# Copying accumulators out of PSUM in their own column order, and undoing the order in the addresses of the stores

## The chip, the cores and the metric

The kernel runs on one core of one Trainium2 chip. The metric is the device time of one launch in microseconds (us). Before the change it is 2262.58 us, the median of three runs (2262.18 to 2262.81).

## The reference, cut to what matters

A light convolution (each of 8 heads has 7 softmaxed taps, applied backwards in time to its 24 channels) is followed by a feed-forward layer with a piecewise quadratic activation:

```python
# x: (8, 4096, 192), weight: (8, 7), w_in: (192, 2048), w_out: (2048, 192), float32
w = softmax(weight, axis=-1)
x_unf = x_pad[:, idx, :].reshape(B, S, K, H, group)          # 7 taps per token
x = einsum('hk,bskhg->bshg', w, x_unf).reshape(B * S, 192)   # 32768 tokens
h = x @ w_in
g = where(h >= 1, h, where(h <= -1, 0, (h + 1) ** 2 / 4))
out = g @ w_out                                              # (32768, 192)
```

## The kernel before, in words

**Tiling.** The 32768 tokens are cut into 64 strips of 512 (TB). The 2048 hidden channels are cut into 8 pairs of 128-channel blocks (NPAIR). A step q is one pair in one strip, so a strip has 8 steps and there are 512 of them. Two strips share one round of the convolution, so the work repeats every 16 steps.

**A step.** The loop over q writes the order of each engine by hand (manual schedule). TensorE (PE) does `mm1(q)`, 18 matmuls on half the rows each, into a double-buffered PSUM tile h; then `mm2(q-2)`, 20 matmuls into the accumulators of its strip. Operands are split into a high and a low part, so mm2 reads two tiles, gh and gl. Between them VectorE (DVE) does `act_clip(q)` (L473), `act_lo(q-1)` (L497, makes gl) and `act_max(q)` (L484); ScalarE (ACT) does `act_hi(q-1)` (L491, makes gh) and `act_square(q)` (L479). The convolution of the strips to come is laid between these: products on ACT (L219), sums on GpSimd (POOL, L230), transpositions on DVE (L147).

**Four accumulators, one set.** A strip sums into four PSUM tiles: accm0 and accm1 for output channels 0 to 127, accr0 and accr1 for channels 128 to 191; the index is the half of the rows that was summed. There is one set, since the pool has one buffer of each. When the last step of a strip has been through mm2, `evac` copies the four tiles to SBUF tiles t on ACT (L513), in the order accm0, accm1, accr0, accr1, and POOL adds each pair (L515). The first mm2 of the next strip writes the same tiles, first accm (8 matmuls from gh, then 4 from gl), then accr. In ACT's own queue the four copies stand behind `act_square` of their step and ahead of `act_hi` of the next.

**Token order.** mm1 and mm2 each read their moving operand by turns from the first and second half of a strip, so the columns of an accumulator are permuted. Column 4a + 2b + o holds token 256b + 128o + a. From strip 2 on (`in_turns`) the copy on ACT undoes this: it reads a PSUM tile in order and writes t with steps of 128 and 256 elements.

**Storing.** Two and three steps into the next strip, `store` transposes the summed tile by blocks of 32 x 32 on DVE into osb (L538) and issues 4 stores for "m" and 2 for "r" from the sync engine's queue (SP, L542), 64 KB each in runs of 32 floats. SP also issues, in the same queue, the loads of x (L95) and the copies that swap partition halves of the convolution's result (L235, L236). Strips 0 and 1 are computed and stored in another way, and strip 63 is emptied by `evac_last`; neither is touched.

Of the kernel before, what the change touches and what calls it, by code (L numbers as in the profile page):

```python
# [20 lines left out]
SQ = 32  # L21
# [9 lines left out]
def lightconv_then_ffn(ctx: ExitStack, tc: tile.TileContext, x, weight, w_in, w_out, out):  # L31
# [24 lines left out]
    nc = tc.nc  # L56
# [343 lines left out]
    def in_turns(s):  # L400
        return s * NPAIR >= NF32
# [99 lines left out]
    def evac(s):  # L501

        acc = accs.pop(s)
        n = slice(0, 2 * D if s * NPAIR < NF32 else TB)
        for a in "mr":
            t = [ob.tile([P, TB], F32, name="t", bufs=4) for _ in range(2)]
            y = ob.tile([P, TB], F32, name="sum")
            for i in range(2):
                to, of = t[i][:, n], acc[a, i][:, n]
                if in_turns(s):  # L510
                    to = to.rearrange("p (b o a) -> p a b o", b=2, o=2)
                    of = of.rearrange("p (a b o) -> p a b o", b=2, o=2)
                nc.scalar.copy(to, of)  # L513
            if s > 0:
                nc.gpsimd.tensor_add(y[:, n], t[0][:, n], t[1][:, n])  # L515
            else:
                late.append((y[:, n], t[0][:, n], t[1][:, n]))
            sums[s, a] = y
# [9 lines left out]
    def store(s, a, *engs):  # L528
        engs = engs or (nc.sync,)
        y = sums.pop((s, a))  # L530
        if s * NPAIR < NF32:
            t0 = s * TB + (0 if a == "m" else 2 * P)
            engs[0].dma_start(out=out[t0:t0 + 2 * P].rearrange("(b p) d -> p b d", p=P),
                              in_=y[:, 0:2 * D].rearrange("p (b d) -> p b d", b=2))
            return
        n = P if a == "m" else DR
        osb = ob.tile([P, TB // SQ, SQ], F32, name="osb")
        nc.vector.transpose(out=osb[0:n].rearrange("p j b -> p (j b)"), in_=y[0:n])  # L538
        for i in range(n // SQ):
            c0 = i * SQ + (0 if a == "m" else P)  # L540
            dst = out[s * TB:(s + 1) * TB, c0:c0 + SQ]
            engs[i % len(engs)].dma_start(out=dst.rearrange("(j a) b -> a j b", a=SQ),  # L542
                                          in_=osb[i * SQ:(i + 1) * SQ])

    def diagonal(t, *bases):
        nc.gpsimd.memset(t, 0.0)
# [293 lines left out]
    for q in range(NQ + DELAY):  # L840
        s, j = divmod(q, NPAIR)
        c, i = divmod(q, 2 * NPAIR)
# [20 lines left out]
        else:  # L863
            if q - 1 in gs:
                act_hi(q - 1)
            if q == NPAIR + 1:
                evac(0)
# [19 lines left out]
            if q < NQ and j == m:  # L887
                evac_rest(s - 1)
                store(s - 1, "m")
            elif q < NQ and j == r:  # L890
                store(s - 1, "r")
# [31 lines left out]
```

## Time and profile before

| what | value |
|---|---|
| median of 3 runs | 2262.58 us |
| the profiled execution | 2263.56 us |
| its span, first to last instruction | 2261.8 us |
| granted TensorE clock | 1.000 |
| busy DVE, ACT, POOL | 92%, 79%, 51% of the span |
| DMA | 110.84 MB, mean 49 GB/s |

The span is what the traces cover; 1.76 us of the profiled execution lie around it. Times in the timelines are us from the start of the span. "PEld" is the loading of TensorE's weights, which runs ahead of the matmuls; a wait of PEld is the matmul's wait seen at its weights. Matmul ends are modelled, so the starts are the figures to use.

### The profile page before, as it was taken

The page shows a single profiled execution, that of the slowest core. Times are in us where ns is not written, and L with a number is a line of the kernel's source. Part 1 is how long each engine was busy: PE and PEld are TensorE (multiplying, and loading weights), DVE is VectorE, ACT ScalarE, POOL GpSimd, SP SyncE. Part 2 cuts the span into 40 slices and gives each one's busy share as a digit, 9 for nine tenths or more (in the row PEclk, how much of TensorE's full clock was granted, in tenths as well). Part 3 has the DMA queues.
Part 4 walks back from the last instruction along what each step waited for, and adds up shares of the span by engine and source line. Part 5 has one row for each costly group of instructions (what it writes and reads, how often), then busy time and mean ns, then how long its engine had stood idle before and what let it go on. Part 6 is the DMA issues. An engine that isn't in the chain of part 4 may idle for free.

```text
span 2261.8 us, 48144 instructions
## 1 busy us (share of the span) xinstructions
PE 2189.4 (97%) x19646; PEld 1862.2 (82%) x19646; DVE 2077.1 (92%) x1883; ACT 1785.3 (79%) x2153; POOL 1148.6 (51%) x868
## 2 busy tenths in 40 slices
PE   9999999999999999999999999999999999999999
PEld 6988888888888888888888888888888888888887
DVE  8899999999999999999999999999999999999998
ACT  7787877778877788777887787877878778788775
POOL 1455644556545565444654455644556445565451
PEclk9999999999999999999999999999999999999999
DMA  6222122221222212222122222222221222212211
GB/s 158 49 51 51 38 53 44 47 53 38 51 48 46 53 34 51 49 49 51 41 44 48 49 50 48 42 48 44 51 53 39 51 49 45 54 34 51 49 32 27
DMA packets 442125, 110.84 MB, mean 49 GB/s; under 512 B 410288, under 2 KB 417840, under 8 KB 441904
## 3 DMA queue, kind: packets, MB, share of 16 engines
q1 hardware_dynamic: 441744, 107.66, 24.2%
q8 instruction: 155, 2.54, 0.5%
q14 instruction: 66, 0.54, 0.1%
q10 hardware_dynamic: 160, 0.10, 0.0%
HBM read 32.84 MB, written 25.17 MB: 26 GB/s over the span
## 4 chain that ended last, share of the span: by engine, by line
DVE 26%; ACT 23%; PE 20%; issue 14%; POOL 12%; SPq 3%; DMA 1%; POOLq 0%; DVEq 0%; ACTq 0%
POOL y L230 11%; PE h L422 9%; DVE g L484 8%; ACT t L513 8%; DVE g L473 8%; DVE gl L497 7%; ACT g L479 6%; ACT gh L491 5%; PE accm L462 5%; PE accr L462 4%; DVE osb L538 2%; SPq L95 2%; ACT p L219 2%; POOL lo L252 2%; DMA raw<-in_x_dram 1%
## 5 line engine op out<-in xcount | busy, mean ns | idle before, releaser
L230 POOL TENSOR_TENSOR y<-y,p 128x512 f32<-128x512 f32 x546 | 799.8, 1465 | 757.9 <-DVE g L484 539.8
L497 DVE TENSOR_TENSOR gl<-g,gh 128x1024 fp32r<-128x1024 f32 (+1 forms) x497 | 727.5, 1464 | 151.4 <-ACT gh L491 140.4
L491 ACT CAST gh<-g 128x1024 fp32r<-128x1024 f32 (+1 forms) x497 | 519.2, 1045 | 253.9 <-DVE g L484 248.7
L422 PE MATMUL h<-hi,w 64*128 64x512 f32 x4032 | 701.6, 377 | 0.0
L479 ACT ACTIVATE g<-g 128x1024 f32<-128x1024 f32 (+1 forms) x505 | 533.6, 1057 | 161.3 <-DVE g L473 151.0
L462 PE MATMUL accm<-gh,w 64*128 64x512 f32 x3968 | 614.0, 381 | 48.0 <-ACT t L513 48.0
L484 DVE TENSOR_TENSOR g<-h,g 128x1024 f32<-128x1024 f32 (+1 forms) x505 | 613.4, 1215 | 8.2 <-ACT g L479 4.4
L473 DVE TENSOR_SCALAR g<-h 128x1024 f32<-128x1024 f32 (+1 forms) x505 | 604.8, 1198 | 11.6 <-PE h L422 10.8
L422 PEld LDWEIGHTS h<-hi,w 64*128 64x128 f32 x4032 | 522.7, 186 | 50.5
L462 PEld LDWEIGHTS accm<-gh,w 64*128 64x128 f32 x3968 | 439.1, 186 | 128.4 <-ACT t L513 78.3
L422 PE MATMUL h<-lo,w 64*128 64x512 f32 x2016 | 541.7, 376 | 0.0
L462 PE MATMUL accr<-gh,wr 64*128 64x512 f32 x1984 | 390.4, 382 | 15.7 <-ACT t L513 15.7
L462 PE MATMUL accm<-gl,w 64*128 64x512 f32 x1984 | 380.0, 382 | 3.2
L219 ACT ACTIVATE p<-xT,wk 128x512 f32<-128x512 f32 x562 | 375.1, 710 | 0.0
L462 PE MATMUL accr<-gl,wr 64*128 64x512 f32 x1984 | 374.1, 376 | 0.0
L422 PEld LDWEIGHTS h<-lo,w 64*128 64x128 f32 x2016 | 330.4, 186 | 25.8
L462 PEld LDWEIGHTS accr<-gh,wr 64*128 64x128 f32 x1984 | 251.9, 186 | 63.0 <-ACT t L513 40.2
L422 PE MATMUL h<-rhi,w 64*128 64x512 f32 x992 | 293.6, 376 | 0.0
L422 PE MATMUL h<-rh,w 64*128 64x512 f32 x992 | 293.5, 376 | 0.0
L462 PEld LDWEIGHTS accm<-gl,w 64*128 64x128 f32 x1984 | 248.6, 186 | 44.3 <-DVE gl L497 23.1
L462 PEld LDWEIGHTS accr<-gl,wr 64*128 64x128 f32 x1984 | 256.8, 186 | 26.1 <-DVE gl L497 0.2
L515 POOL TENSOR_TENSOR sum<-t 128x512 f32<-128x512 f32 (+1 forms) x124 | 158.5, 1279 | 153.3 <-ACT t L513 153.3
(141 smaller groups left out, 2008.6 us busy)
## 6 DMA issues: line engine op xcount, KB each, us to landing
out_dram<-osb SPq DMA_DIRECT2D x366, 64.0 KB, 1.9
raw<-in_x_dram SPq DMA_DIRECT2D x334, 68.0 KB, 2.4
hi<-hi SPq DMA_DIRECT2D x126, 128.0 KB, 2.3
lo<-lo SPq DMA_DIRECT2D x126, 128.0 KB, 2.3
rhi<-rh SPq DMA_DIRECT2D x62, 128.0 KB, 2.2
rlo<-rl SPq DMA_DIRECT2D x62, 128.0 KB, 2.3
words<-in_moe_w_in_dram SPq DMA_DIRECT2D x16, 192.0 KB, 4.0
words<-in_moe_w_out_dram SPq DMA_DIRECT2D x8, 384.0 KB, 4.0
```

Of the source, the lines that this page charges most:

```text
L95: (engs[i] if engs else nc.sync).dma_start(out=raw[i * SQ:(i + 1) * SQ, lo:n // SQ + 1, :], in_=src.rearrange("(j a) b -> a j b", a=SQ),)
L219: nc.scalar.mul(p, self.xT[:, SH + k:SH + k + TB], wk[:, self.wsel, k:k + 1])
L230: nc.gpsimd.tensor_add(y, y, self.product(k))
L422: nc.tensor.matmul(to, w[HALVES[e], c0:c0 + P], of, start=(n == 0), stop=(n == len(mms) - 1))
L462: nc.tensor.matmul(both(accs[s][a, i]), st, turns(g[HALVES[i], e, :]), start=(j == 0 and n == first[a]), stop=(j == NPAIR - 1 and n == las ...
L473: nc.vector.tensor_scalar(out=g[:, e, :], in0=hs[q][:, e, :], scalar1=-1.0, scalar2=1.0, op0=ALU.max, op1=ALU.min)
L479: nc.scalar.activation(g[:, e, :], g[:, e, :], AF.Square, bias=0.5, scale=0.5)
L484: nc.vector.tensor_tensor(out=g[:, e, :], in0=h[:, e, :], in1=g[:, e, :], op=ALU.max)
L491: nc.scalar.copy(gh[:, e, :], gs[q][:, e, :])
L497: eng.tensor_sub(gl[:, e, :], g[:, e, :], gh[:, e, :])
L513: nc.scalar.copy(to, of)
L515: nc.gpsimd.tensor_add(y[:, n], t[0][:, n], t[1][:, n])
```

## The change

The copies out of PSUM no longer rearrange: they read 512 columns and write 512 columns, both in order. The sum, the small add in `evac_rest` and the 32 x 32 transposition therefore work on permuted tokens. With a = 8j + k (k from 0 to 7, j from 0 to 15) and e = 2b + o, column 4a + e is column 4k + e of transposition block j, so partition 4k + e of osb holds, in block j, token 128e + 8j + k. The address of the store is written in those terms.

```diff
             for i in range(2):
-                to, of = t[i][:, n], acc[a, i][:, n]
-                if in_turns(s):
-                    to = to.rearrange("p (b o a) -> p a b o", b=2, o=2)
-                    of = of.rearrange("p (a b o) -> p a b o", b=2, o=2)
-                nc.scalar.copy(to, of)
+                nc.scalar.copy(t[i][:, n], acc[a, i][:, n])
...
             dst = out[s * TB:(s + 1) * TB, c0:c0 + SQ]
-            engs[i % len(engs)].dma_start(out=dst.rearrange("(j a) b -> a j b", a=SQ),
-                                          in_=osb[i * SQ:(i + 1) * SQ])
+            engs[i % len(engs)].dma_start(
+                out=dst.rearrange("(e j k) b -> k e j b", e=4, k=SQ // 4),
+                in_=osb[i * SQ:(i + 1) * SQ])
```

No instruction is added, removed or moved on any engine. What differs is the shape of 244 copies on ACT (128x128x4 before, 128x512 now) and of 366 stores on SP. The rows below are SP's queue in the middle of a round of two strips, before: two swaps of the low part (lo), the stores of a strip, then the swaps of the remaining channels (rh, rl).

```order
L235 DMA lo_2523<-lo_2517 64x512
L236 DMA lo_2523<-lo_2517 64x512
L542 DMA out_dram<-osb 32x16x32 x6
L235 DMA rhi<-rh 64x512
L236 DMA rhi<-rh 64x512
L235 DMA rlo<-rl 64x512
```

The same place with the change:

```order
L235 DMA lo_2523<-lo_2517 64x512
L236 DMA lo_2523<-lo_2517 64x512
L538 DMA out_dram<-osb 8x64x32 x6
L235 DMA rhi<-rh 64x512
L236 DMA rhi<-rh 64x512
L235 DMA rlo<-rl 64x512
```

The order is the same. The address side of a store was 32 rows of 16 runs, and is now 8 rows (k) of 64 runs, since e and j together form one even step of 8 tokens; each run is 32 floats in both. The osb side stays 32 partitions of 512 floats.

## The prediction

> **What bounds the kernel now.** I read the busy row first, then the table of waits, then the timeline of one round of two strips.
>
> ```profile
> PE 2189.4 (97%) x19646; PEld 1862.2 (82%) x19646; DVE 2077.1 (92%) x1883; ACT 1785.3 (79%) x2153; POOL 1148.6 (51%) x868
> ```
>
> PE is the bound by this row, and DVE is close behind. ACT, on which the copies run, has room on average. What matters is where PE stops:
>
> ```profile
> DVE gl L497 <- ACT gh L491: 140.4, 106, 2.2
> ...
> PEld accm L462 <- ACT t L513: 78.3, 91, 1.2
> ...
> PEld accr L462 <- ACT t L513: 40.2, 61, 0.7
> PEld accm L462 <- DVE gl L497: 23.1, 58, 0.5
> ```
>
> The copies (L513) hold up the weight loads of mm2 for 78.3 + 40.2 = 118.5 us: the next strip cannot start before the four accumulators are copied. The 61 waits for accr are one per strip change that the change touches (strips 2 to 62). The copies also stand ahead of gh in ACT's queue, and most of DVE's idle time, 140.4 us, is waiting for gh.
>
> One round, PE. The first row opens the step in which a new strip begins (I call this strip change A); then the two restarts, and the openings of the next two steps.
>
> ```profile
> 1001.83 0.81 PE L422 MATMUL h<-hi,w 64*128 64x512 f32 x4
> 1004.66 1.13 PE L462 MATMUL accm<-gh,w 64*128 64x512 f32 x7 [0.41 <-ACT t L513]
> 1006.48 0.70 PE L462 MATMUL accr<-gh,wr 64*128 64x512 f32 x3 [0.26 <-ACT t L513]
> 1007.23 0.80 PE L422 MATMUL h<-hi,w 64*128 64x512 f32 x4
> 1011.33 0.80 PE L422 MATMUL h<-hi,w 64*128 64x512 f32 x4
> ```
>
> An undisturbed step takes 1011.33 - 1007.23 = 4.10 us. Step A takes 5.40: 1.30 are lost. The other strip change of the round (B), eight steps on:
>
> ```profile
> 1036.70 0.59 PE L422 MATMUL h<-hi,w 64*128 64x512 f32 x4
> 1039.60 0.48 PE L462 MATMUL accm<-gh,w 64*128 64x512 f32 x1 [0.80 <-ACT t L513]
> 1040.51 1.13 PE L462 MATMUL accm<-gh,w 64*128 64x512 f32 x7 [0.42 <-ACT t L513]
> 1042.32 0.70 PE L462 MATMUL accr<-gh,wr 64*128 64x512 f32 x3 [0.25 <-ACT t L513]
> 1043.07 0.80 PE L422 MATMUL h<-hi,w 64*128 64x512 f32 x4
> 1071.78 0.81 PE L422 MATMUL h<-hi,w 64*128 64x512 f32 x4
> ```
>
> Step B takes 6.37, so 2.27 are lost. From A to the next A are 1071.78 - 1001.83 = 69.95 us, where 16 undisturbed steps would take 65.6. Of the 4.35 us lost, 3.57 are at A and B; the rest, about 0.8, lies in the heavy half between them, where DVE is late with gl:
>
> ```profile
> 1022.85 0.30 PEld L462 LDWEIGHTS accm<-gl,w 64*128 64x128 f32 x4 [0.53 <-DVE gl L497]
> ```
>
> **The copies.** Groups of copies on ACT, by shape: count, busy us and mean ns.
>
> ```profile
> L513 ACT COPY t<-accr 128x512 f32<-128x512 f32 x122 | 123.0, 1113 | 0.0
> L513 ACT COPY t<-accm 128x512 f32<-128x512 f32 x122 | 118.9, 1079 | 0.0
> ...
> L202 ACT COPY hi<-accm 128x512 f32<-128x512 f32 x1 | 0.6, 586 | 1.4 <-PE accm L181 1.4
> ...
> L198 ACT COPY rh<-accr 128x512 f32<-128x512 f32 x1 | 0.6, 572 | 0.0
> ```
>
> L202 and L198 are the operation that the change makes of L513: a copy of 512 floats from PSUM to SBUF, both sides in order. They take 0.58 us against 1.10. Only two samples, but strip 0 copies its accumulators in order too, 384 columns wide, at a time when PE runs:
>
> ```profile
> 58.51 0.83 ACT L513 COPY t<-accm 128x384 f32<-128x384 f32 x2
> 59.24 0.86 ACT L513 COPY t<-accr 128x384 f32<-128x384 f32 x2
> 60.02 1.06 ACT L479 ACTIVATE g<-g 128x1024 f32<-128x1024 f32 x1
> ```
>
> Four take 1.51 us from start to start, 0.38 each for some 0.47 of duration: neighbours overlap by about 0.1. So four of 0.58 should take 4 x 0.485 = 1.94 us. At A and B the rows now are:
>
> ```profile
> 1002.66 1.95 ACT L513 COPY t<-accm 128x512 f32<-128x512 f32 x2
> 1004.42 2.01 ACT L513 COPY t<-accr 128x512 f32<-128x512 f32 x2
> 1006.23 1.05 ACT L491 CAST gh<-g 128x1024 fp32r<-128x1024 f32 x1
> ...
> 1038.51 1.95 ACT L513 COPY t<-accm 128x512 f32<-128x512 f32 x2
> ```
>
> Today four take 1006.23 - 1002.66 = 3.57 us, so each strip change gives ACT 1.63 us back. Bounds for a copy: 0.57 (L198) and 1.11 (no change); I take 0.58.
>
> **What PE gets at A.** A step is 38 matmuls in 4.10 us, 0.108 each, so mm1 (18) is over, and accm wanted, 1.94 us after the step opens: 1003.77. The second copy will end at 1002.66 + 0.49 + 0.58 = 1003.73, so accm is free just in time. accr is wanted 12 matmuls (1.29 us) later, at 1005.06; the fourth copy ends at 1002.66 + 3 x 0.485 + 0.58 = 1004.70. All 1.30 us go. This is tight for accm: 0.1 us more per copy would bring 0.15 us of the wait back at each A.
>
> **What PE gets at B.** The copies start late here, at 1038.51, as ACT is kept by convolution work. accm is wanted at 1036.70 + 1.94 = 1038.64; the second copy ends at 1038.51 + 0.49 + 0.58 = 1039.58, with some 0.06 until PE moves. About 1.0 us stays, and 1.27 go. Everything ahead of B will have moved up together by then, so the lateness of ACT at B stays as it is. accr is then no longer late.
>
> **What DVE gets.** Its rows behind A and B, and POOL's sums at A:
>
> ```profile
> 1007.31 1.55 DVE L497 TENSOR_TENSOR gl<-g,gh 128x1024 fp32r<-128x1024 f32 x1 [1.91 <-ACT gh L491]
> ...
> 1011.66 2.31 DVE L497 TENSOR_TENSOR gl<-g,gh 128x1024 fp32r<-128x1024 f32 x1
> ...
> 1043.15 1.56 DVE L497 TENSOR_TENSOR gl<-g,gh 128x1024 fp32r<-128x1024 f32 x1 [2.01 <-ACT gh L491]
> ...
> 1004.68 1.28 POOL L515 TENSOR_TENSOR sum<-t 128x512 f32<-128x512 f32 x1 [2.89 <-ACT t L513]
> 1006.50 1.28 POOL L515 TENSOR_TENSOR sum<-t 128x512 f32<-128x512 f32 x1 [0.54 <-ACT t L513]
> ```
>
> gh comes 1.63 us sooner, inside both waits (1.91, 2.01), so DVE moves forward too. Not by all of it: gl takes 2.31 where POOL works beside it and 1.55 where the second sum covers its first 0.47 us. The sums also move up, to about 1003.8 and 1005.1, and the second will cover some 0.7 us of gl: I charge 0.15, and leave DVE 1.5. That is 0.2 more than PE's 1.30, and takes 0.2 from the wait for gl in the heavy half. The sums themselves, the transposition and the small add keep their sizes; nobody waits for them sooner.
>
> **The stores.** Six per strip, still 64 KB in 512 runs of 32 floats; only the addresses' steps differ. I cost them at nothing. Their landing is covered by the time until the same osb buffer is written again, one strip (35 us); their issue by the gaps in SP's queue. Bounds: unchanged, or, if 8 rows were worse than 32, a few times the landing and the issue of now; the price without cover is the last rival below.
>
> **Sum.** Per round 1.30 + 1.27 + 0.2 = 2.77 us; 61 strip changes are 30.5 rounds, 84.5 us. 2263.56 - 84.5 = 2179.1 for the profiled execution; the median shown is 0.98 below it, so **2178 us**.
>
> **Rivals.** *The sums cost DVE more.* If gl is slowed at each strip change to the longest row, 2.31 instead of 1.55, DVE keeps only 1.63 - 0.76 = 0.87 and PE must follow: 61 x 0.87 = 53, 2210 us. For it: DVE is 92% busy. Against: the overlap worked out is short. Chance 0.15.
>
> *All of the loss goes.* DVE's lead grows until ACT is on time at B and gl on time in the heavy half. PE would run 16 undisturbed steps: 4.35 x 30.5 = 133, 2130 us at best. The round's busy row speaks against the full sum:
>
> ```profile
> 1002.66:1072.66 70.00, 67.74 (x612) 57.46 (x611) 64.72 (x57) 55.82 (x68) 37.03 (x29) 1.00 0.24 47
> ```
>
> DVE (third figure behind the length) needs 64.72 of the 65.6, and still waits a little for gh. I put this case at 2130 to 2160. Chance 0.15.
>
> *The copies stay slow.* The price may be in the reading while PE writes other banks, not in the scattered writing. Then nothing moves: 2262. Strip 0's copies speak against it. [...] Chance 0.05.
>
> *Slower: stores that hold the transfer engines.* The swaps of rh and rl are issued behind the stores in the same queue and must land before mm1 of the next round:
>
> ```profile
> 1046.49 5.94 SPq L542 DMA_DIRECT2D out_dram<-osb  x6
> ...
> 1059.72 0.59 SPq L236 DMA_DIRECT2D rlo<-rl  x1
> ...
> 1065.30 0.38 PE L422 MATMUL h<-rl,w 64*128 64x512 f32 x1
> ...
> out_dram<-osb SPq DMA_DIRECT2D x366, 64.0 KB, 1.9
> ...
> rlo<-rl SPq DMA_DIRECT2D x62, 128.0 KB, 2.3
> ```
>
> The last swap lands at 1060.31 + 2.3 = 1062.6, 2.7 us before its matmul. The last store is issued by 1052.43; were it to hold the engines beyond 1065.30 - 2.3 = 1063.0, that is 10.6 us after its issue instead of 1.9, the swap behind it would be late for PE. Each us beyond costs 31 us, once a round, and from 2178 + 31 x 2.7 on, at 13.3 us, the kernel is slower than before (2283 at 14 us). Issue is no danger by itself: at twice the 5.94 us SP would be done at 1058.4, still some 2 us inside the swaps' margin. What the new shape could do to the landing: if the 512 runs went over half of the 16 engines, each would carry 64 and not 32, and twice 1.9 is 3.8 us, far from 10.6. The page "DMA: Bandwidth & Descriptors" (section Why a DMA increments its semaphore by 16 and not by 1) says that a copy uses the largest number of engines up to 16 that divides the slowest dimension of both sides: 16 for 32 rows, 8 for 8 rows; no row of before shows a store of 8 rows. Chance 0.03.
>
> **How the numbers follow.** The forecast has 0.62, within 2165 to 2195. With the cases of more (2130 to 2160) and of less (2195 to 2225), a range of 2143 to 2215 leaves out some 0.2. A difference of 0.2%, some 4.5 us, is about what a measurement of this kernel can tell from none. Faster 0.92, same 0.05, slower 0.03.
>
> **What would show it.** The copies at 0.58 us, and ACT's busy time down by 244 x 0.52 = 127 us; accr no longer waiting for t, accm still for about 1.0 us at every B (some 30 us); the wait of gl for gh down from 140 by up to 1.63 x 61 = 99; a round of 67.2 us; the stores' landing under 4 us. It would be wrong if the copies stayed above 0.8 us, if gl behind the strip changes took over 2 us, or if B kept or lost its whole wait.

## The result, and the profile after

The changed kernel takes **2169.9 us** (median of four runs, 2169.37 to 2170.33), against 2262.69 for the kernel before on the same chip: a ratio of 0.959 with a 95% interval of 0.9573 to 0.9606. It is 92.8 us faster, of which the prediction had 84.5. The profiled execution took 2170.33 us and has a span of 2168.6.

First the busy row of the profile after. The row has the same columns as the one of before:

```profile
PE 2153.0 (99%) x19646; PEld 1875.8 (86%) x19646; DVE 2084.0 (96%) x1883; ACT 1684.8 (78%) x2153; POOL 1139.4 (53%) x868
```

PE now stops for 1% of the span instead of 3%, with as many instructions as before. DVE has come up to 96%. ACT lost 100.5 us of work. The table of waits, after (engine, tile and line, whom it waited for: us in total, times, longest):

```profile
DVE gl L497 <- ACT gh L491: 41.3, 110, 0.6
...
PEld accm L462 <- ACT t L509: 29.4, 58, 0.7
...
PEld accm L462 <- DVE gl L497: 12.3, 54, 0.3
```

The 40.2 us of accr waiting for a copy have no row any more. accm's wait fell from 78.3 to 29.4, DVE's for gh from 140.4 to 41.3. The groups of copies by shape, after:

```profile
L509 ACT COPY t<-accr 128x512 f32<-128x512 f32 x122 | 66.4, 606 | 0.0
L509 ACT COPY t<-accm 128x512 f32<-128x512 f32 x122 | 64.5, 580 | 0.0
```

So 580 and 606 ns stand where 1079 and 1113 stood. PE's timeline at the strip change A, at B, and the step behind each, after:

```profile
962.73 0.81 PE L422 MATMUL h<-hi,w 64*128 64x512 f32 x4
...
964.67 1.24 PE L462 MATMUL accm<-gh,w 64*128 64x512 f32 x8
...
966.83 0.80 PE L422 MATMUL h<-hi,w 64*128 64x512 f32 x4
...
995.94 0.59 PE L422 MATMUL h<-hi,w 64*128 64x512 f32 x4
...
998.37 1.61 PE L462 MATMUL accm<-gh,w 64*128 64x512 f32 x8 [0.32 <-ACT t L509]
...
1000.90 0.80 PE L422 MATMUL h<-hi,w 64*128 64x512 f32 x4
```

Step A takes 966.83 - 962.73 = 4.10 us: nothing is lost there now. Step B takes 1000.90 - 995.94 = 4.96: 0.86 of its 2.27 remain. ACT's timeline at the two places:

```profile
963.55 1.06 ACT L509 COPY t<-accm 128x512 f32<-128x512 f32 x2
964.49 1.10 ACT L509 COPY t<-accr 128x512 f32<-128x512 f32 x2
965.45 1.08 ACT L491 CAST gh<-g 128x1024 fp32r<-128x1024 f32 x1
...
995.80 1.03 ACT L491 CAST gh<-g 128x1024 fp32r<-128x1024 f32 x1
996.78 1.06 ACT L479 ACTIVATE g<-g 128x1024 f32<-128x1024 f32 x1
997.75 1.05 ACT L509 COPY t<-accm 128x512 f32<-128x512 f32 x2
```

Four copies take 965.45 - 963.55 = 1.90 us from start to start. At B they start 997.75 - 995.94 = 1.81 us after the step opens, exactly as late as before (1038.51 - 1036.70). DVE's timeline, first behind A, then in the heavy half, then around B:

```profile
966.56 1.75 DVE L497 TENSOR_TENSOR gl<-g,gh 128x1024 fp32r<-128x1024 f32 x1 [0.26 <-ACT gh L491]
...
971.10 2.12 DVE L497 TENSOR_TENSOR gl<-g,gh 128x1024 fp32r<-128x1024 f32 x1
...
995.54 1.21 DVE L473 TENSOR_SCALAR g<-h 128x1024 f32<-128x1024 f32 x1
...
1000.75 2.04 DVE L497 TENSOR_TENSOR gl<-g,gh 128x1024 fp32r<-128x1024 f32 x1 [0.39 <-ACT gh L491]
```

gl waits 0.26 and 0.39 us for gh where it waited 1.91 and 2.01, but it takes longer itself: 1.75 instead of 1.55 behind A, 2.04 instead of 1.56 behind B. One round, by engine, after (the columns are those of the prediction's row: the stretch and its length, then the busy us of PE, PEld, DVE, ACT and POOL with their instructions, the clock, the DMA share and GB/s):

```profile
962.73:1029.61 66.88, 66.55 (x611) 57.55 (x609) 64.88 (x57) 52.45 (x67) 36.59 (x29) 1.00 0.26 49
```

A round is 66.9 us instead of 69.95, with DVE busy for 64.88 of them: its idle time per round has gone from 70.00 - 64.72 = 5.28 to 66.88 - 64.88 = 2.00 us.

### The profile page after: what moved, and what is told of

Its sections match the earlier page's. It is cut to its first block, busy times and chain, and to the rows that moved or that the text cites. A ratio compares the mean times of both kernels' runs of the same rounds, so it can differ in the third digit from the quotient of the medians.

```text
span 2168.6 us, 48144 instructions
## 1 busy us (share of the span) xinstructions
PE 2153.0 (99%) x19646; PEld 1875.8 (86%) x19646; DVE 2084.0 (96%) x1883; ACT 1684.8 (78%) x2153; POOL 1139.4 (53%) x868
## 3 DMA queue, kind: packets, MB, share of 16 engines
q1 hardware_dynamic: 438816, 107.65, 25.9%
## 4 chain that ended last, share of the span: by engine, by line
DVE 27%; PE 24%; ACT 19%; POOL 13%; issue 13%; SPq 3%; DMA 1%; POOLq 0%; DVEq 0%; ACTq 0%
POOL y L230 11%; PE h L422 10%; DVE g L484 9%; DVE g L473 8%; PE accm L462 7%; DVE gl L497 7%; ACT g L479 6%; ACT gh L491 5%; PE accr L462 4%; ACT t L509 4%; DVE osb L534 2%; SPq L95 2%; ACT p L219 2%; POOL lo L252 2%; DMA raw<-in_x_dram 1%
## 5 line engine op out<-in xcount | busy, mean ns | idle before, releaser
L497 DVE TENSOR_TENSOR gl<-g,gh 128x1024 fp32r<-128x1024 f32 (+1 forms) x497 | 734.4, 1478 | 51.6 <-ACT gh L491 41.3
L479 ACT ACTIVATE g<-g 128x1024 f32<-128x1024 f32 (+1 forms) x505 | 535.1, 1060 | 167.3 <-DVE g L473 157.0
L473 DVE TENSOR_SCALAR g<-h 128x1024 f32<-128x1024 f32 (+1 forms) x505 | 604.7, 1198 | 11.6 <-PE h L422 10.6
L462 PE MATMUL accm<-gh,w 64*128 64x512 f32 x3968 | 604.2, 378 | 9.3 <-ACT t L509 9.1
L422 PEld LDWEIGHTS h<-hi,w 64*128 64x128 f32 x4032 | 523.7, 186 | 47.9
L462 PEld LDWEIGHTS accm<-gh,w 64*128 64x128 f32 x3968 | 449.4, 186 | 77.0 <-ACT t L509 29.4
L462 PE MATMUL accr<-gh,wr 64*128 64x512 f32 x1984 | 373.4, 376 | 0.0
L462 PEld LDWEIGHTS accm<-gl,w 64*128 64x128 f32 x1984 | 250.9, 186 | 33.4 <-DVE gl L497 12.3
L462 PEld LDWEIGHTS accr<-gh,wr 64*128 64x128 f32 x1984 | 257.3, 186 | 24.7 <-ACT gh L491 0.2
L422 PEld LDWEIGHTS h<-rhi,w 64*128 64x128 f32 x992 | 184.5, 186 | 14.9
```

What stands on the lines that cost most here:

```text
L422: nc.tensor.matmul(to, w[HALVES[e], c0:c0 + P], of, start=(n == 0), stop=(n == len(mms) - 1))
L462: nc.tensor.matmul(both(accs[s][a, i]), st, turns(g[HALVES[i], e, :]), start=(j == 0 and n == first[a]), stop=(j == NPAIR - 1 and n == las ...
L473: nc.vector.tensor_scalar(out=g[:, e, :], in0=hs[q][:, e, :], scalar1=-1.0, scalar2=1.0, op0=ALU.max, op1=ALU.min)
L479: nc.scalar.activation(g[:, e, :], g[:, e, :], AF.Square, bias=0.5, scale=0.5)
L497: eng.tensor_sub(gl[:, e, :], g[:, e, :], gh[:, e, :])
```

## The experiments

Three questions were put: whether the gain is all of the copies and nothing of the stores; what it is in a copy that costs; and why B still loses 0.86 us, since the prediction had given a reason for that ("ACT is kept by convolution work") that no row had proved.

The table gives, for every version, the median, the ratio to the kernel before on the same chip with its interval, and where a round stands: the lengths of step A, of the two late steps of the heavy half, of step B, and of the round. The steps are read from the starts of mm1 in PE's weight queue, in one round between 960 and 1100 us, so they may differ by 0.02 from the matmul rows above. Rounds differ little, but for B in e6, where both of its lengths are given.

| kernel | median us | ratio | A | heavy | heavy, 2nd | B | round |
|---|---|---|---|---|---|---|---|
| before | 2262.69 | 1 | 5.41 | 4.73 | 4.25 | 6.37 | 69.95 |
| after | 2169.9 | 0.959 [0.9573, 0.9606] | 4.11 | 4.36 | 4.27 | 4.96 | 66.89 |
| e1, stores alone | 2263.2 | 1.0001 [0.9991, 1.001] | 5.42 | 4.67 | 4.26 | 6.37 | 69.92 |
| e2, copies alone | 2170.2 | 0.9589 [0.9575, 0.9603] | 4.10 | 4.34 | 4.26 | 4.96 | 66.85 |
| e3, m in order | 2212.42 | 0.9776 [0.9761, 0.979] | 4.57 | 4.67 | 4.25 | 5.57 | 68.26 |
| e4, r in order | 2215.01 | 0.9787 [0.9773, 0.9802] | 4.61 | 4.40 | 4.25 | 5.85 | 68.30 |
| e6, no sums | 2145.19 | 0.9478 [0.9464, 0.9492] | 4.11 | 4.10 | 4.10 | 4.86 or 4.23 | 66.37 or 65.7 |
| e7, products later | 2173.17 | 0.96 [0.9585, 0.9614] | 4.10 | 4.31 | 4.25 | 5.02 | 66.88 |
| e9, m first | 2164.94 | 0.9565 [0.9549, 0.9581] | 4.10 | 4.23 | 4.25 | 4.83 | 66.62 |
| e8, e7 and e9 together | 2188.82 | 0.9667 [0.9653, 0.9682] | 4.62 | 4.46 | 4.23 | 4.31 | 67.32 |
| e11, one product later, m first | 2159.07 | 0.9542 [0.9526, 0.9558] | 4.10 | 4.18 | 4.26 | 4.70 | 66.45 |
| e10, strided read | 2170.84 | 0.9589 [0.9573, 0.9605] | 4.10 | 4.40 | 4.28 | 4.96 | 66.93 |

### The stores alone

The kernel before with the new addresses of the stores, and the copies as they were:

```diff
-            engs[i % len(engs)].dma_start(out=dst.rearrange("(j a) b -> a j b", a=SQ),
-                                          in_=osb[i * SQ:(i + 1) * SQ])
+            engs[i % len(engs)].dma_start(
+                out=dst.rearrange("(e j k) b -> k e j b", e=4, k=SQ // 4),
+                in_=osb[i * SQ:(i + 1) * SQ])
```

> The old copies with the new stores; the rows of each strip land in another order within the strip. Theory (all of the gain is the copies; the stores are hidden): 2262 us, within 0.1% of before, with an issue of 0.68 us per store instead of 0.49 and the step pattern of before. Rival (part of the difference is the stores: better because a store's pieces lie 6 KB apart instead of 24 KB, or worse because it goes over fewer engines): off by more than 5 us, either way.

It took 2263.2 us, and its steps are those of before. SP's issues of the stores (least, median and longest ns of one) and the queue's packets in this kernel:

```profile
L542 SPq DMA_DIRECT2D out_dram<-osb x366: 675/676/1774, 136.5 to 2236.6; - x183
...
q1 hardware_dynamic: 438816, 107.65, 24.8%
```

And of the kernel before:

```profile
L542 SPq DMA_DIRECT2D out_dram<-osb x366: 315/488/2030, 137.1 to 2237.5; - x183
...
q1 hardware_dynamic: 441744, 107.66, 24.2%
```

A store of the new shape takes SP 0.19 us longer to issue, and there are 441744 - 438816 = 2928 packets less, 8 for each of the 366 stores, for the same bytes. Both are hidden, as the time shows. The eight packets fit the Trainium skill, "DMA: Bandwidth & Descriptors" (section Why a DMA increments its semaphore by 16 and not by 1): every engine that takes part in a copy ends its share with a write to the semaphore, and by the rule that the prediction drew from the same section, 8 slowest rows leave 8 engines instead of 16. By that page the packets agree; the runs show no engine by name.

### The copies alone

The kernel after, with the stores' addresses of before:

```diff
-            engs[i % len(engs)].dma_start(
-                out=dst.rearrange("(e j k) b -> k e j b", e=4, k=SQ // 4),
-                in_=osb[i * SQ:(i + 1) * SQ])
+            engs[i % len(engs)].dma_start(out=dst.rearrange("(j a) b -> a j b", a=SQ),
+                                          in_=osb[i * SQ:(i + 1) * SQ])
```

> The new copies with the old stores; the rows of each strip land in another order within the strip. Theory: 2170 us, the time of the full change within 0.1%. Rival (the new stores cost something that the copies' gain covers): faster than 2165.

2170.2 us. The whole gain is that of the copies, and the slower rival (stores that hold the transfer engines) falls with these two runs.

### One pair of copies in order

The kernel before, with `m` in order and `r` scattered (e3); for e4 the condition is `a != "r"`. The store of each pair has the address that belongs to its copies (not shown).

```diff
                 to, of = t[i][:, n], acc[a, i][:, n]
-                if in_turns(s):
+                if in_turns(s) and a != "m":
                     to = to.rearrange("p (b o a) -> p a b o", b=2, o=2)
                     of = of.rearrange("p (a b o) -> p a b o", b=2, o=2)
...
```

> Only accm0 and accm1 are copied in order (and stored by the new addresses), accr0 and accr1 as before. Theory (each scattered copy costs PE where its tile is wanted, and DVE through gh): step A loses about 0.5 us, on accr, step B about 1.5; 1.6 us less per round, 2214 us. Rival (only the tiles wanted first matter): 2170 to 2185. Rival (only the length of all four copies matters, through DVE): the same time as the kernel with accr alone in order, 2216.

> Only accr0 and accr1 are copied in order, accm0 and accm1 as before. Theory: PE still waits for accm as before (0.7 us at A, 1.9 at B) and no longer for accr; 1.45 us less per round, 2218 us. Rival (only the tiles wanted first matter): 2255 to 2262. Rival (only the length of all four copies matters): the same as with accm alone.

2212.42 and 2215.01 us, against 2262.94 for the kernel before on their chip: each pair is worth about half (50.5 and 47.9 us). With that the rival falls by which only the tiles wanted first matter. The other rival, that only the length of all four copies matters, wants the same time from both, and 2.6 us between them would hardly refute it; the waits do. With m in order, the table of waits of e3:

```profile
PEld accr L462 <- ACT t L513: 39.6, 61, 0.7
PEld accm L462 <- ACT t L513: 30.1, 59, 0.7
```

With r in order, that of e4 has no row for accr:

```profile
PEld accm L462 <- ACT t L513: 76.0, 90, 1.2
```

So accr's wait goes with the r copies and some 48 us of accm's with the m copies, and each leaves about 0.5 us at A. The two gains add up to 98, a little over the 92.8 of both, so they share something; what, was not separated.

### What in a copy costs

The copies of strip s have the form s % 6: in order; single floats scattered (as before); an in-order write of a strided read, which restores the token order; and writes in runs of 2, 4 and 8 floats. It ran once (2188.57 us) and serves for the durations alone; the rows of its output are permuted in most strips.

```diff
+                f = s % 6 if in_turns(s) else 0
...
+                elif f == 2:
+                    nc.scalar.copy(to.rearrange("p (b o a) -> p b o a", b=2, o=2),
+                                   of.rearrange("p (a b o) -> p b o a", b=2, o=2))
+                elif f == 3:
+                    nc.scalar.copy(to.rearrange("p (b a o) -> p a b o", b=2, o=2),
+                                   of.rearrange("p (a b o) -> p a b o", b=2, o=2))
...
```

> The changed kernel, with six forms of the copy in turn by strip: in order; every float to its restored place (as before); the same order restored by reading PSUM in steps of 4 floats and writing in order; and writing runs of 2, 4 and 8 floats to two places in turn. Most strips then land in another order, so only the durations count. Theory (the price of the old copy lies in writing single floats far apart): in order and strided reading both at 0.58 to 0.62 us, the old form at 1.08 to 1.11, runs of 2 in between, runs of 4 and 8 at 0.6. Rival (it lies in reading by a pattern of several steps): every form but the first at about 1.1.

The copies of accr by their line, in the groups of this kernel (L512 in order, L514 scattered, L517 strided read, L520, L523 and L526 runs of 2, 4 and 8):

```profile
L514 ACT COPY t<-accr 128x512 f32<-128x512 f32 x20 | 20.2, 1114 | 0.0
...
L517 ACT COPY t<-accr 128x512 f32<-128x512 f32 x22 | 11.9, 605 | 0.0
L520 ACT COPY t<-accr 128x512 f32<-128x512 f32 x20 | 11.8, 662 | 0.0
...
L526 ACT COPY t<-accr 128x512 f32<-128x512 f32 x20 | 10.9, 606 | 0.0
L523 ACT COPY t<-accr 128x512 f32<-128x512 f32 x20 | 10.9, 605 | 0.0
L512 ACT COPY t<-accr 128x512 f32<-128x512 f32 x20 | 10.9, 604 | 0.0
```

In these copies only the writing costs, and only below 4 floats at a place: 1114 ns for single floats, 662 for pairs, 604 to 606 for everything else. Reading PSUM with steps of 4 floats took 605, no longer than in order.

### The same gain without touching the stores

That gives another way to the same end. The kernel before, with its stores, and one word order changed in the copies:

```diff
-                    to = to.rearrange("p (b o a) -> p a b o", b=2, o=2)
-                    of = of.rearrange("p (a b o) -> p a b o", b=2, o=2)
+                    to = to.rearrange("p (b o a) -> p b o a", b=2, o=2)
+                    of = of.rearrange("p (a b o) -> p b o a", b=2, o=2)
```

> The kernel before with its own stores; the copy still restores the token order, but reads PSUM in steps of 4 floats and writes SBUF in order. Theory (only the scattered writing was dear): copies at 0.58 to 0.61 us and 2170 us, as the full change. Rival (reading in steps holds PE's writes to PSUM or costs elsewhere): above 2175.

2170.84 us: the same time as after, to 0.05%. The permutation was never the price, only the side on which it was done.

### POOL's sums beside DVE

gl takes longer in many places where POOL works beside it. Here the sums of strips 2 to 62 are left out (the first half of the rows alone is stored):

```diff
-            y = ob.tile([P, TB], F32, name="sum")
+            y = t[0] if in_turns(s) else ob.tile([P, TB], F32, name="sum")
...
             if s > 0:
-                nc.gpsimd.tensor_add(y[:, n], t[0][:, n], t[1][:, n])
+                if not in_turns(s):
+                    nc.gpsimd.tensor_add(y[:, n], t[0][:, n], t[1][:, n])
...
```

> The changed kernel without POOL's sums of the two accumulator halves (the first half alone is stored), in strips 2 to 62. Theory (the sums, moved up by the change, slow gl on DVE at every strip change): gl behind the strip changes falls from 1.75 and 2.04 to about 1.2 us, the lost quarter us of the heavy half goes, B shrinks by some 0.3, 2150 us. Rival (POOL beside DVE costs PE nothing): 2170.

2145.19 us, 24.7 less than after, and the heavy half loses nothing. The row of gl among the groups of after, then of this kernel:

```profile
L497 DVE TENSOR_TENSOR gl<-g,gh 128x1024 fp32r<-128x1024 f32 (+1 forms) x497 | 734.4, 1478 | 51.6 <-ACT gh L491 41.3
```

```profile
L497 DVE TENSOR_TENSOR gl<-g,gh 128x1024 fp32r<-128x1024 f32 (+1 forms) x497 | 665.5, 1339 | 40.8 <-ACT gh L491 34.3
...
L473 DVE TENSOR_SCALAR g<-h 128x1024 f32<-128x1024 f32 (+1 forms) x505 | 606.3, 1201 | 46.5 <-PE h L422 46.3
```

DVE has 69 us less to do for gl, and its clip (L473) now waits 46.3 us for PE, where it waited 10.6 after. So the sums cost this kernel about 25 us, through DVE. The Trainium skill, "SBUF — State Buffer" (section Who interferes with whom), has a rule for it: a VectorE instruction with two inputs in SBUF gets the second through a port that it shares with GpSimd's reads, and one with at most one SBUF input, outside the two-port modes, does not contend. gl, with two, agrees; L473, which reads PSUM, stays at 1.2 us in both kernels.

What is left on POOL then takes longer, the small add in `evac_rest` above all (after: 1292 ns each; the names of its tiles are exchanged here):

```profile
L523 POOL TENSOR_TENSOR t<-t,sum 64x512 f32<-64x512 f32 x61 | 137.5, 2255 | 19.3 <-ACT sum L522 19.3
```

So the run takes contention off DVE in part by moving it to POOL, which has the time, and 25 us is the price of the sums where they stand, not of all contention.

B is of two kinds in this run. Of 29 rounds it takes 4.75 to 4.95 us in 14 and 4.22 to 4.27 in the other 15, and one row tells them apart in every round: the third gl behind A. Here it is, with POOL's addition beside it, ahead of a B of 4.86 and of one of 4.23:

```profile
1033.58 1.90 DVE L497 TENSOR_TENSOR gl<-g,gh 128x1024 fp32r<-128x1024 f32 x1
1033.12 1.28 POOL L230 TENSOR_TENSOR y<-y,p 128x512 f32<-128x512 f32 x1
...
1099.97 1.20 DVE L497 TENSOR_TENSOR gl<-g,gh 128x1024 fp32r<-128x1024 f32 x1
1099.52 2.79 POOL L230 TENSOR_TENSOR y<-y,p 128x512 f32<-128x512 f32 x1
```

POOL starts 0.45 us ahead of gl in both. Once DVE is slowed, by 0.7 us, and once POOL is, by 1.5. When POOL bears it, the first copy at B starts 1.28 us after the step opens instead of 1.92, and B loses next to nothing. The kernel after has one such round in 29: there the second gl behind A takes 1.20 us in place of 2.1, the heavy half loses nothing, and B takes 4.57. So POOL's work beside DVE, of which the sums are a part, also sets how much B loses. What decides which of the two engines is slowed, these rows don't show.

### Why B is late: the convolution's products

The prediction said that ACT is kept by convolution work there. In this kernel the three products that ACT computes in the step ahead of B (`8: (0, 1, 2)`) come two steps later, and the four behind them one step each:

```diff
-    PLAN_R = {7: ("T",), 8: (0, 1, 2), 10: (3, 4), 11: (5, 6), 13: "split"}
+    PLAN_R = {7: ("T",), 10: (0, 1, 2), 11: (3, 4), 12: (5, 6), 13: "split"}
```

> The changed kernel with the three products of the remaining channels, which ACT computes just ahead of B, put into the steps behind B. Theory of the prediction (at B the copies start late because convolution work keeps ACT): the copies start up to 1.3 us sooner, B loses next to nothing, 2145 us. Rival (ACT waits for DVE there: its square starts 0.03 us after the clip of its step has ended): B loses its 0.86 us as now, 2168 to 2172.

2173.17 us, and B is 5.02: no gain. ACT's timeline at B in this kernel:

```profile
1063.04 1.05 ACT L491 CAST gh<-g 128x1024 fp32r<-128x1024 f32 x1 [1.66 <-DVE g L484]
1064.18 1.06 ACT L479 ACTIVATE g<-g 128x1024 f32<-128x1024 f32 x1
1065.14 1.05 ACT L509 COPY t<-accm 128x512 f32<-128x512 f32 x2
```

And DVE's:

```profile
1062.88 1.21 DVE L473 TENSOR_SCALAR g<-h 128x1024 f32<-128x1024 f32 x1
```

ACT now stands idle for 1.66 us ahead of the gh of the step before, and still the copies are late: they stand behind the square (L479), the square reads what the clip (L473) writes, and the clip ends at 1062.88 + 1.21 = 1064.09, just ahead of 1064.18. After, the same holds: the clip of 995.54 ends at 996.75, the square starts at 996.78. It is DVE that is late at B, as the two kinds of B in e6 also show, and ACT passes it on.

### The copies ahead of the square

If so, copies that need not wait for the square should help. At B the m copies are issued ahead of `act_hi`, the r copies stay behind the square:

```diff
...
+            split = i == 9 and NPAIR < done < NQ - 1
+            if split:
+                evac(done // NPAIR, "m")
...
-                (evac if done < NQ - 1 else evac_last)(done // NPAIR)
+                if split:
+                    evac(done // NPAIR, "r")
+                else:
+                    (evac if done < NQ - 1 else evac_last)(done // NPAIR)
```

> The changed kernel with the copies of accm0 and accm1 put ahead of gh in ACT's queue at B alone (accr stays behind the square). Theory (at B the copies stand behind a gh and a square that are late through DVE): PE's wait at B goes, 0.86 us a round, but gh and so DVE are up to 0.9 us later there, of which the light half takes back some 0.6; 2145 to 2165 us. Rival (DVE is the bound of the whole round): 2180 or more.

2164.94 us, 5 less than after, and B 4.83. The waits of this kernel:

```profile
PEld accm L462 <- DVE gl L497: 39.4, 89, 1.0
```

In its timeline PE's weight queue at B:

```profile
1064.21 0.30 PEld L462 LDWEIGHTS accm<-gl,w 64*128 64x128 f32 x4 [0.79 <-DVE gl L497]
```

PE no longer waits for a copy, but of the 0.86 us that B lost, 0.73 are there again as a wait for gl, which has grown from 12.3 us in all to 39.4. ACT's timeline and DVE's say why:

```profile
1060.64 1.05 ACT L509 COPY t<-accm 128x512 f32<-128x512 f32 x2
1061.59 1.05 ACT L491 CAST gh<-g 128x1024 fp32r<-128x1024 f32 x1
...
1062.67 1.49 DVE L497 TENSOR_TENSOR gl<-g,gh 128x1024 fp32r<-128x1024 f32 x1 [1.08 <-ACT gh L491]
```

gh now stands behind the two copies, which take ACT 0.95 us, and gl waits 1.08 us for it. The copies' place was changed, and another wait took theirs.

### Both, and a milder form of both

> Both edits at B together: the three products behind B, and the copies of accm0 and accm1 ahead of gh. Theory (at B PE waits on a chain DVE, ACT, DVE; ACT is idle for 1.65 us ahead of gh once the products are gone, so the two copies cost that chain some 0.5 us instead of 1.1): B loses 0.2 to 0.4 us instead of 0.73, 2150 to 2158 us. Rival (the copies' place is worth only what it was worth alone): 2165.

The two edits together missed: 2188.82 us. B did fall to 4.31, but the light half, which nothing had disturbed, lost about 0.5 us (steps of 4.36, 4.20 and 4.45, of which steps of 4.01 and 3.99 take back 0.2), A 0.5 and the first late step of the heavy half 0.1 more than after. The waits that are long in this kernel:

```profile
ACT rh L262 <- POOL y L230: 37.9, 29, 1.3
...
ACT t L509 <- PE accm L462: 40.2, 31, 2.8
```

ACT is held twice a round: by copies that are issued before PE is through, and by the convolution's result, which comes late from POOL. The first kind alone is next to nothing in e9 (3.4 us), and the second alone, with the same 37.9 us in e7, cost nothing; which of the two, or that they meet, makes the light half lose was not separated. A milder form moves the products by one at a time, and keeps m first:

```diff
-    PLAN_R = {7: ("T",), 8: (0, 1, 2), 10: (3, 4), 11: (5, 6), 13: "split"}
+    PLAN_R = {7: ("T",), 8: (0, 1), 10: (2, 3), 11: (4, 5), 12: (6,), 13: "split"}
...
```

> As the kernel with both edits, but only one of the three products goes behind B, and the others are spread so that POOL's last sum comes a step sooner. Theory (the time lost behind B was the chain from the late products over POOL's sums to rh, and that chain has slack again): the light half runs at 4.10 us per step, B loses about 0.5, 2150 to 2160 us. Rival (any work of ACT put behind B is paid for there): 2165 to 2185.

2159.07 us (2158.85 to 2159.21), the fastest version of all that compute the whole reference: 0.5% below the change, 4.6% below the kernel before. B takes 4.70 and the light half loses nothing; ACT's wait for the convolution's result is gone. What is left in its table of waits is DVE, and at B gl both waits for gh and takes long itself:

```profile
PEld accm L462 <- DVE gl L497: 36.5, 89, 0.8
...
1059.49 1.86 DVE L497 TENSOR_TENSOR gl<-g,gh 128x1024 fp32r<-128x1024 f32 x1 [0.58 <-ACT gh L491]
```

## Why the prediction was right, point by point

**The price of the copies.** 0.58 us from two rows elsewhere in the program, 0.580 and 0.606 measured; four in 1.94 us, 1.90 measured. That the cost lay in the scattered writing, which the rival "the copies stay slow" doubted, e5 shows. ACT's busy time fell by 100.5 and not by 127 us: busy time counts overlapping neighbours once, so the fall is 61 times the 3.57 - 1.90 = 1.67 us by which four copies shrank, 102.

**A.** All of 1.30 us went, as worked out, and accm was free just in time. e3 and e4, where either pair is still slow, leave 0.5 there: both pairs were needed, as the two restarts in PE's rows said.

**B.** 1.41 us went where 1.27 were predicted. The start of the copies was right to 0.01 us (1.81 after the step opens). The term was mis-sized at PE's restart: the prediction let all eight matmuls wait for the second copy, 2.94 us after the opening. PE starts at 998.37, after 2.43, as soon as the first copy is through, and the eight then take 1.61 us, 0.37 more than at A: part of the wait lies between them. They end as if all had started 2.80 after the opening, and that 0.14 is what the term was short.

**The reason given for what stays at B** was wrong. "The copies start late here, as ACT is kept by convolution work" falls with e7, in which ACT waits idle and B stays late; the chain of clip, square and copies behind a late DVE takes its place. ACT's own queue comes next: with the copies ahead of the square (e9), gh behind them makes gl late, and only then does moving convolution work shorten B (to 4.31 in e8). The forecast didn't suffer, since it needed only that the lateness would stay. That it stayed was luck as far as the reason goes: that all ahead of B "will have moved up together" holds in most rounds of after, but where one gl ran beside POOL unslowed, B took 4.57 instead of 4.96.

**The heavy half.** 0.2 us were predicted back, 0.35 came: 4.70 to 4.35 (the table's one round has 4.73 to 4.36). The prediction let DVE gain 0.2 us on PE at A; it gained 1.65 - 0.20 - 1.30 = 0.15, and the long gl there is 2.12 instead of 2.31 us, which was not foreseen. The two together make 0.34.

**What DVE gives back.** 0.15 us per strip change were charged for POOL's sums, 0.20 and 0.48 came. The term was too small, at B by a factor of three, and one of the prediction's own signs of being wrong came true there: gl behind B takes 2.04 us, over the 2 that it had named. The rival "the sums cost DVE more" had 0.76 at every strip change, and e6 puts 25 us on the sums as a whole. The time held all the same, since gl waits 1.65 and 1.62 us less for gh, and DVE gave up 3.3 us of idle time per round.

**The stores** at nothing: shown by e1 and e2. Whether they land in under 4 us stays open, as no trace of a kernel with the new stores gives a landing. One wait for a store, by POOL near the very end, is all that shows of it: 5.5 us after, and 5.1 in e2, which has the old stores.

Together: 1.30 + 1.41 + 0.35 = 3.06 us per round, 30.5 rounds, 93.3 us, against 93.2 between the two profiled executions. The forecast was short by 0.29 us a round, 8.8 us, in the terms of B and of the heavy half. The rival "all of the loss goes" wanted 4.35 a round; 1.3 stay, and e6 and e7 put them on DVE and on what POOL does beside it.

## What to carry to other kernels

When a ScalarE copy out of PSUM has to permute, do it on the side that is read, or write in runs of at least 16 bytes: both were free here, the first with steps of 4 floats. Price such a copy by who waits for its tile and by what is queued behind it: ACT was busy for 79% of the span, and still 0.5 us on each of 244 copies cost the kernel 4%. When a wait names an engine, look whether that engine was idle ahead of the instruction: ACT was named at B, and the cause was two steps up its chain, in a DVE instruction that POOL slowed. What is saved on one engine comes back as a wait for the next one in the chain, so the last microseconds were found here by moving a few instructions at a time.

## What the runs showed of the hardware

- An ACT copy of 512 floats per partition (accr's, in e5) took 604 ns to write in order, 605 in runs of 4, 662 in runs of 2, and 1114 as single floats; a PSUM read with a step of 4 floats cost nothing (605).
- accr's copies took 25 to 27 ns longer than accm's of the same shape, and 30 to 38 where single floats or pairs were written; no run says why.
- A VectorE subtraction with both inputs in SBUF took 1.2 us alone and up to 2.1 (2.3 before) beside GpSimd's additions. In e6 it sometimes kept its 1.2 us, and then the addition beside it took 2.79 us in place of 1.28.
- A store with 8 rows of 64 runs took SP 676 ns to issue, one with 32 rows of 16 runs 488, with the same bytes and the same length of run.
